# An attention and routed-experts kernel: the last head's row of maxima turned one place later, routing steps moved behind the last maxima, and the ramp's order changed

## The chip, the cores and the metric

The kernel runs on one core of one Trainium2 chip. Its time is the device time of one execution in microseconds (us). A core has five engines that run side by side and wait for each other through semaphores: TensorE (PE) multiplies matrices and writes into PSUM; VectorE (DVE), ScalarE (ACT) and GpSimd (POOL) work element by element; SyncE (SP) issues transfers (DMA). Each engine does its instructions in the order in which the program lists them.

## The reference

Three parts follow each other. Attention with 2 x 8 heads of 768 rows and 64 columns, in which a row sees only the columns of its own hash bucket:

```python
q_bits = (np.einsum('bhsd,dk->bhsk', q, proj) > 0); k_bits = ...   # 6 bits each
mask = q_bucket[:, :, :, None] == k_bucket[:, :, None, :]
scores = np.where(mask, scale * np.matmul(q, k.transpose(0, 1, 3, 2)), -1e9)
attn = np.exp(scores - max); attn = attn / (sum + 1e-9); out = np.matmul(attn, v)
```

Then each of the 1536 rows (512 wide) is routed to one of 8 experts by the largest gate logit and goes through relu(x w1) w2 of that expert; then a layer h = x w_in, h * clip(h + 3, 0, 6) / 6, times w_out.

## The kernel before, in words

The program is written out for each engine in a fixed order by Python code; nothing reorders it. Attention runs in 96 steps k, six for each of 16 heads; step k = 6 h + j treats 128 keys of head h. In a step, `scores(k)` makes on PE two halves of 128 x 384 scores (pst, two matmuls each: high times high parts, then the low parts together with the bits and the row of maxima) and on ACT the exp of each (pf). `high(k)` copies pf to fp16 (phi), nearly always on ACT; `low(k)` makes the remainder pf - phi (plo), on GpSimd, in the last two heads mostly on VectorE. `pv(k)` multiplies phi and plo by the values (psv, 36 matmuls for two steps); it is done for two steps together in each odd step, four and five steps late. `mx(n)` makes, eight steps ahead, the maxima that the exp of a later head needs: two matmuls (psm, three PSUM tiles in turn) and a VectorE reduction (mx) of each. After a head's sixth `mx` a small reduction makes top, and `turn` transposes it on PE (pstop), casts it on VectorE (rm), and sends it as a row by DMA into X, where `scores` of that head reads it. The buffers pf are four: the exp of step k waits until plo of step k - 4 is done.

What else must happen in attention is a list of small steps with due times (`at`, `spread`, `stages`): the head's split into parts (`prep`), sign bits (`bits`, psb on PE, b on VectorE), the scale of each group of four heads (`vmax`, `vscale`: psn and pso on PE, then a chain of tiny VectorE operations am, ex, sc, isw), the splitting of values (`vsplit`, vh), the gate columns (`vgate`: psg, gv), a head's output (`evac`: rd, xp), and the routing of the first half (`route(0)`: ge, jo, pl, jt, rh, ohr; `weigh(0)`: se, gt, rg). A due time of 15 stands between the steps 14.5 and 15; `due(k - 0.5)` runs ahead of the step's scores and `due(k)` behind its sums of values. The table Q holds most of these times. Q["ac"] says how many `mx` the first eight steps do, Q["hn"] how many idle heating matmuls (`heat`, zeros times zeros) stand behind the scores of a step. The ramp is the part before the main loop (scores of steps 0 and 1, the first `vscale`) with the first steps of the loop.

Of the kernel before, what the change touches and what calls it, by code (L numbers as in the profile page):

```python
# [23 lines left out]
NC = S // P  # L24
# [21 lines left out]
LEAD = 8  # L46
# [17 lines left out]
def moe_attention_kernel(ctx, tc, qk, v, vt, pj, wg, w1, w2, win, wout, out, cap):  # L64
# [246 lines left out]
    Q = {'tk': (84, 86), 'v': (-3.25, -4.75, -1.75, -2.25), 'vg': (-6.5, -6.75), 'vgd': 1, 'pr': (-13.0, -12.75, -12.0, -12.5), 'prd': 0.6, 'b0': 7.75, 'b': 1.75, 'bd': 0.5, 'vm0': (9.5, 10.5, 11.5, 12.5), 'vm': (-0.5, 4.75, 7.0, 12.25), 'vs': 13.25, 'pa': 1.5, 'ev': 0.5, 'lvt': -5.0, 'v4': (2.0, 4.25, 10.0, 16.25), 'vg0': (1.85, -4.4, 9.0), 'p2': 3.5, 'lr': (0.25, 1.25, 2.25), 'lv': 4.0, 'vsd': 0.75, 'ac': (1, 1, 3, 5, 6, 7, 8, 10), 'hd': (3, 5, 17), 'hn': (0, 0, 3, 2, 2, 1, 0, 0), 'ap': (0,), 'h0': (7,), 'hl': (6,), 'l0': (), 'll': (1, 3), 'ht': (6, 3, 7, 6, 3, 2)}  # L311
# [4 lines left out]
    with ExitStack() as actx:  # L316
# [486 lines left out]
        run(vs)  # L803
        heat(ps_v, "v", 2)
# [45 lines left out]
        stages(first[1], (2, 3, 3.5, 4, 4.5))  # L850
# [3 lines left out]
        for g in range(1, G):  # L854
            b = 4 * NC * (g - 1)
            spread(b + Q["b"] + (g == 2) if g > 1 else Q["b0"], bits(g), Q["bd"])
            at(b - 6 if g > 1 else Q["lv"], load_v, g)
            for i in range(4):
                at(b + (Q["vm"] if g > 1 else Q["vm0"])[i], vmax, g, i)
            if g == 1:  # L860
                stages(vscale(g), (13, 14.5, 15.25, 16.75, 17.5))
            else:
                spread(b + Q["vs"], vscale(g))
# [19 lines left out]
        stages(route(0, lambda: misc("psr0")), [66 + 1.5 * i for i in range(8)] + [84.5 + 0.75 * i for i in range(14)])  # L883
# [13 lines left out]
        for k in range(STEPS + LAG + 2):  # L897
            due(k - 0.5)
            if 1 < k <= STEPS and not on_dve(k - 1):
                high(k - 1, act)  # L900
            if 1 < k < STEPS:
                scores(k)
# [683 lines left out]
```

## Time and profile before

| | |
|---|---|
| timed runs | 661.88, 658.0, 662.19 us; median 661.88 |
| the profiled execution | 658.55 us, of which the span of its instructions is 656.8 |
| mean granted clock of TensorE | 0.985 of full |
| busy: PE, DVE, ACT, POOL | 96%, 73%, 66%, 36% of the span |
| attention | from the start to about 226 us |
| hand-over to the experts (routing, first gathers) | about 226 to 239 us |

A row of a timeline says when an instruction (or several alike, "x6") began, how long it was busy, its engine, line and operation, "what it writes<-what it reads", the size, and in brackets how long its engine had been idle before it and who released it. A busy PE is not a PE at its peak: its clock has two levels, 1.00 (2.4 GHz) and 0.50 (1.2 GHz) of the granted clock.

### The profile page before, as it was taken

How to read it: one execution, taken by the hardware profiler on the slowest of the kernel's cores; microseconds unless marked ns; L12 is line 12 of the kernel's file. 1: busy time of each engine (PE TensorE's matmuls, PEld its weight loads, DVE VectorE, ACT ScalarE, POOL GpSimd, SP SyncE). 2: the span in 40 equal slices, each digit the busy share in tenths (PEclk: the TensorE clock that was granted, in tenths of full speed). 3: DMA queues.
4: the chain of work that ended last, by engine and by line, in shares of the span. 5: the costliest groups of instructions: out<-in, count | busy, mean ns of one | idle time of the engine just before them, and what ended most of it. 6: DMA issues, size and time to landing. Idle time of an engine off the chain costs nothing.

```text
span 656.8 us, 14463 instructions
## 1 busy us (share of the span) xinstructions
PE 627.4 (96%) x5529; PEld 456.8 (70%) x5529; DVE 477.0 (73%) x1056; ACT 436.6 (66%) x882; POOL 236.0 (36%) x221
## 2 busy tenths in 40 slices
PE   8899999999998889999999999999999999999893
PEld 3578788888887669999999995555555555555441
DVE  6689899998998888888888887888888342222420
ACT  8768878888886847777776755455555586555730
POOL 6567978988995052110666300000000030000011
PEclk9899999999996999999999999999999999999998
DMA  5647758746464168777677643444341010000011
GB/s 195 202 109 222 196 129 230 193 128 164 116 187 157 28 203 300 247 248 230 215 250 258 205 138 107 142 150 139 129 132 61 1 64 33 1 0 1 1 49 53
DMA packets 35732, 92.19 MB, mean 140 GB/s; under 512 B 6778, under 2 KB 12250, under 8 KB 35650
## 3 DMA queue, kind: packets, MB, share of 16 engines
q1 hardware_dynamic: 32562, 83.75, 42.4%
q0 software_dynamic: 2400, 7.36, 3.3%
q8 instruction: 46, 0.75, 0.4%
q14 instruction: 36, 0.29, 0.1%
q10 hardware_dynamic: 688, 0.03, 0.1%
HBM read 67.14 MB, written 6.29 MB: 112 GB/s over the span
## 4 chain that ended last, share of the span: by engine, by line
PE 55%; ACT 3%; DVE 3%; DMA 2%; issue 1%; POOL 0%; POOLq 0%; DVEq 0%
PE psg L1360 17%; PE pso L1387 15%; PE psy L1138 11%; PE psh L1111 11%; DMA out_dram<-os,inv 2%; ACT junk L1314 2%; PE psa L1088 1%; ACT gh L1370 1%; DVE wl L164 1%; DVE rl L1363 1%; ACT rl L1362 0%; PE heat L1190 0%; DVE hl L1115 0%; POOL out_dram L1402 0%; ACT wh L158 0%
## 5 line engine op out<-in xcount | busy, mean ns | idle before, releaser
L493 POOL TENSOR_TENSOR plo<-pf,phi 128x768 f16<-128x768 f32 x86 | 147.0, 1734 | 21.6 <-ACT phi L487 8.1
L1402 POOL DMA_INDIRECT out_dram<-os,inv x12 | 12.2, 1014 | 270.7 <-DVE os L1394 244.3
L482 ACT ACTIVATE pf<-pst 128x384 f32<-128x384 f32 x192 | 83.5, 486 | 37.6 <-PE pst L481 34.6
L459 DVE TENSOR_REDUCE mx<-psm 128x1 f32<-128x384 f32 x192 | 96.2, 546 | 12.4 <-PE psm L456 12.0
L164 DVE SCALAR_TENSOR_TENSOR wl<-raw,wh 128x1024 f16<-128x1024 f32 (+1 forms) x68 | 82.4, 1215 | 6.0 <-ACT wh L158 5.2
L1360 PE MATMUL psg<-yTh,ch 128*128 128x512 f16 (+1 forms) x256 | 83.4, 326 | 3.2 <-DVE rl L1363 3.2
L1360 PE MATMUL psg<-yTl,ch 128*128 128x512 f16 (+1 forms) x256 | 83.4, 326 | 0.0
L1360 PE MATMUL psg<-yTh,cl 128*128 128x512 f16 (+1 forms) x256 | 83.4, 326 | 0.0
L1363 DVE SCALAR_TENSOR_TENSOR rl<-rl,psg 128x512 f32<-128x512 f32 x64 | 35.0, 551 | 64.4 <-ACT rl L1362 64.0
L480 PE MATMUL pst<-Y,K 128*128 128x384 f32 x192 | 76.4, 398 | 2.1 <-ACT pf L482 2.0
L1360 PEld LDWEIGHTS <-ch 128*128 128x128 f16 x512 | 50.1, 98 | 35.9
L487 ACT ACTIVATE phi<-pf 128x768 f16<-128x768 f32 x85 | 71.7, 843 | 1.9
L1387 PE MATMUL pso<-ch,gh 128*128 128x512 f16 x192 | 72.8, 379 | 0.0
L1387 PE MATMUL pso<-ch,gl 128*128 128x512 f16 x192 | 72.8, 379 | 0.0
L1387 PE MATMUL pso<-cl,gh 128*128 128x512 f16 x192 | 72.8, 379 | 0.0
L158 ACT ACTIVATE wh<-raw 128x1024 f16<-128x1024 f32 (+1 forms) x68 | 67.4, 998 | 0.8 <-DVE offs L987 0.8
L481 PE MATMUL pst<-X,K 77*128 77x384 f32 x192 | 66.8, 348 | 0.6 <-DMA X<-rm 0.6
L1387 PEld LDWEIGHTS <-gh 128*128 128x128 f16 x384 | 37.6, 98 | 42.3
L1138 PE MATMUL psy<-hh,wl 128*128 128x224 f16 x256 | 66.3, 259 | 0.2 <-DVE wl L164 0.2
L1138 PE MATMUL psy<-hh,wh 128*128 128x224 f16 x256 | 66.3, 259 | 0.0
L1138 PE MATMUL psy<-hl,wh 128*128 128x224 f16 x256 | 66.3, 259 | 0.0
L508 PE MATMUL psv<-vh,phi 128*128 128x73 f16 x576 | 65.7, 200 | 0.0
(250 smaller groups left out, 1484.7 us busy)
## 6 DMA issues: line engine op xcount, KB each, us to landing
raw<-in_w_dram SPq DMA_DIRECT2D x64, 512.0 KB
rc<-in_win_dram SPq DMA_DIRECT2D x16, 512.0 KB
rc<-in_wout_dram SPq DMA_DIRECT2D x16, 512.0 KB
r<-in_qk_dram SPq DMA_DIRECT2D x16, 384.0 KB
K<-hi SPq DMA_DIRECT2D x26, 192.0 KB
vr<-in_v_dram SPq DMA_DIRECT2D x4, 768.0 KB
vt<-in_vt_dram SPq DMA_DIRECT2D x8, 384.0 KB
K<-lo SPq DMA_DIRECT2D x16, 192.0 KB
```

What stands on the lines that cost most here:

```text
L158: act.activation(wh[e, i][:, c : c + n], r, AF.Copy, scale=(S1, S2)[i // 2])
L164: dve.scalar_tensor_tensor(out=wl[e, i][:, c : c + n], in0=r, scalar=(S1, S2)[i // 2], in1=wh[e, i][:, c : c + n], op0=ALU.mult, op1=ALU.s ...
L459: dve.tensor_reduce(out=mm[:, c, n : n + 1], in_=ps[:, :HS], axis=AX.X, op=ALU.max)
L480: pe.matmul(ps[:, :HS], st["K1"][:, kc], st["Y"][:, qc], start=True, stop=False)
L481: pe.matmul(ps[:, :HS], st["K2"][0:77, kc], st["X"][0:77, qc], start=False, stop=True)
L482: act.activation(pf[:, qc], ps[:, :HS], AF.Exp, scale=0.125 / SC / SC)
L487: act.activation(phi_t[k], pf_t[k], AF.Copy)
L493: eng.tensor_tensor(out=plo_t[k], in0=pf_t.pop(k), in1=phi_t[k], op=ALU.subtract)
L1111: pe.matmul(ps, l[:, c], r[:, k], start=n == 0, stop=n == 3 * KD - 1)
L1138: pe.matmul(ps, l, r, start=n == 0, stop=n == 3 * KF - 1)
L1360: pe.matmul(ps, l, x, start=n == 0, stop=n == 3 * KD - 1)
L1387: pe.matmul(po[blk][s], l, r, start=first and n == 0, stop=last and n == 2)
```

## The change

Six things change, all of them the place of instructions, except for one tiny copy and one more heating matmul in all. (1) `turn` of the last head (n = 95, done in step 87) stands behind that step's `pv` and no longer ahead of it. (2) The steps of `route(0)` from jo on are due later, so that they stand behind the last maxima. (3) A copy of isw onto itself on GpSimd, queued behind the first scale. (4) In the ramp the maxima are spread 1, 2, 2 over steps 2 to 4 in place of 2, 2, 1; the gate columns are made half a step earlier; heating goes from 2 to 1 matmul in steps 3 and 4, and three heating matmuls come ahead of `scores` of step 6. (5) `vscale` of group 1 is due later (13, 15, ...). (6) `bits` of group 2 are due one step earlier.

```diff
--- before.py
+++ after.py
@@ -308,7 +308,7 @@
                 )
 
 
-    Q = {..., 'ac': (1, 1, 3, 5, 6, 7, 8, 10), ..., 'hn': (0, 0, 3, 2, 2, 1, 0, 0), ...}
+    Q = {..., 'ac': (1, 1, 2, 4, 6, 7, 8, 10), ..., 'hn': (0, 0, 3, 1, 1, 1, 0, 0), ...}
 
 
     HT = Q["ht"]
@@ -801,6 +801,7 @@
         next(vs)
         next(vs)
         run(vs)
+        pool.tensor_copy(isw, isw)
         heat(ps_v, "v", 2)
         mx(NC)
         run(pre[1])
@@ -847,18 +848,18 @@
                 at(k, next, gen, None)
 
         stages(first[0], (2, 2))
-        stages(first[1], (2, 3, 3.5, 4, 4.5))
+        stages(first[1], (2, 2.5, 3, 3.5, 4.5))
         at(5.0, run, pre[2])
         for i in range(3):
             at(Q["lr"][i], load_r, 5 + i)
         for g in range(1, G):
             b = 4 * NC * (g - 1)
-            spread(b + Q["b"] + (g == 2) if g > 1 else Q["b0"], bits(g), Q["bd"])
+            spread(b + Q["b"] if g > 1 else Q["b0"], bits(g), Q["bd"])
             at(b - 6 if g > 1 else Q["lv"], load_v, g)
             for i in range(4):
                 at(b + (Q["vm"] if g > 1 else Q["vm0"])[i], vmax, g, i)
             if g == 1:
-                stages(vscale(g), (13, 14.5, 15.25, 16.75, 17.5))
+                stages(vscale(g), (13, 15, 15.75, 17, 17.75))
             else:
                 spread(b + Q["vs"], vscale(g))
         for h in range(8, NH):
@@ -880,7 +881,7 @@
             elif h < NH - 1:
                 at(k + Q["pa"], pair, h // 2)
                 at(NC * h + (-1.9 if h > 1 else -3.5), load_vt, h // 2 + 1)
-        stages(route(0, lambda: misc("psr0")), [66 + 1.5 * i for i in range(8)] + [84.5 + 0.75 * i for i in range(14)])
+        stages(route(0, lambda: misc("psr0")), [66 + 1.5 * i for i in range(8)] + [84.5, 85.25, 87.25, 87.75] + [88.25 + 0.67 * i for i in range(10)])
         stages(weigh(0), (84, 86, 87.25, 88.5, 90.5, 91.5, 92.5))
         stages(any_unmatched(), (88.5, 91, 93.5))
         for i in range(4):
@@ -898,6 +899,8 @@
             due(k - 0.5)
             if 1 < k <= STEPS and not on_dve(k - 1):
                 high(k - 1, act)
+            if k == NC:
+                heat(ps_v, "v", 3)
             if 1 < k < STEPS:
                 scores(k)
             if k < 8 and Q["hn"][k]:
@@ -912,11 +915,11 @@
             for n in AHEAD[k] if k < len(AHEAD) else (k + LEAD,):
                 if n < STEPS:
                     mx(n)
-                if n == STEPS - 1:
-                    turn(turns.pop())
             for u in (k - LAG - 1, k - LAG) if k % 2 else ():
                 if 0 <= u < STEPS:
                     pv(u)
+            if k + LEAD == STEPS - 1:
+                turn(turns.pop())
             due(k)
         assert not later
         for q in range(4):
```

GpSimd at the end of the ramp's preparation, before, and then now (names carry the head or step as their first number; plo0 is the remainder of step 0, vh0 the values of head 0):

```order
L392 TENSOR_TENSOR lo1_242<-rs1_243,hi1_240 128x768
L493 TENSOR_TENSOR plo0_412<-pf0_331,phi0_340 128x768
L733 TENSOR_TENSOR vh0_426<-vr0_179,vh0_426 128x6x64
L493 TENSOR_TENSOR plo1_452<-pf1_349,phi1_397 128x768
L493 TENSOR_TENSOR plo2_483<-pf2_399,phi2_439 128x768
L493 TENSOR_TENSOR plo3_514<-pf3_441,phi3_470 128x768
```

```order
L392 TENSOR_TENSOR lo1_242<-rs1_243,hi1_240 128x768
L804 COPY isw_75<-isw_75 128x1
L493 TENSOR_TENSOR plo0_413<-pf0_331,phi0_340 128x768
L733 TENSOR_TENSOR vh0_421<-vr0_179,vh0_421 128x6x64
L493 TENSOR_TENSOR plo1_448<-pf1_349,phi1_398 128x768
L493 TENSOR_TENSOR plo2_478<-pf2_400,phi2_436 128x768
```

The copy of isw stands ahead of plo0, so plo0 and all behind it wait for the last operation of the scale on VectorE.

PE in the loop's steps 2 and 3, from the second `mx` of head 1 on, before, and then now (psm1cn is half n of chunk c of head 1's maxima, pst3n the scores of step 3, psg0 the gate columns):

```order
L456 MATMUL psm110_414<-K21_145,X1_142 128x384
L456 MATMUL psm111_417<-K21_145,X1_142 128x384
L456 MATMUL psm120_420<-K21_145,X1_142 128x384
L456 MATMUL psm121_423<-K21_145,X1_142 128x384
L571 MATMUL psg0_431<-vt0_182,wg_sb_74 32x256 x3
L480 MATMUL pst30_442<-Y0_139,K10_140 128x384
L481 MATMUL pst30_442<-X0_138,K20_141 128x384
L480 MATMUL pst31_446<-Y0_139,K10_140 128x384
L481 MATMUL pst31_446<-X0_138,K20_141 128x384
L335 LDWEIGHTS idle_sb_135
L335 MATMUL heatv_408<-idle_sb_135 128x512
L335 LDWEIGHTS idle_sb_135
```

```order
L456 MATMUL psm110_415<-K21_145,X1_142 128x384
L456 MATMUL psm111_418<-K21_145,X1_142 128x384
L571 MATMUL psg0_426<-vt0_182,wg_sb_74 32x256 x3
L480 MATMUL pst30_439<-Y0_139,K10_140 128x384
L481 MATMUL pst30_439<-X0_138,K20_141 128x384
L480 MATMUL pst31_443<-Y0_139,K10_140 128x384
L481 MATMUL pst31_443<-X0_138,K20_141 128x384
L335 LDWEIGHTS idle_sb_135
L335 MATMUL heatv_409<-idle_sb_135 128x512
L456 MATMUL psm120_450<-K21_145,X1_142 128x384
L456 MATMUL psm121_453<-K21_145,X1_142 128x384
L456 MATMUL psm130_456<-K21_145,X1_142 128x384
```

Two matmuls of maxima (chunk 2) moved from ahead of the scores of step 3 to behind them, and one heating matmul went.

VectorE at the last maxima (psm1550 and psm1551, chunk 5 of head 15), before, and then now (mx0 and jo are the routing's, se0 the gate's sum, rd13 begins the output of head 13):

```order
L459 TENSOR_REDUCE mx1_161<-psm1540_4179 128x1
L459 TENSOR_REDUCE mx1_161<-psm1541_4182 128x1
L253 TENSOR_REDUCE mx0_3309<-ge0_4163 128x6
L254 TENSOR_TENSOR jo_107<-ge0_4163 128x24
L284 TENSOR_REDUCE se0_4187<-ex0_4103 128x6
L459 TENSOR_REDUCE mx1_161<-psm1550_4202 128x1
L459 TENSOR_REDUCE mx1_161<-psm1551_4205 128x1
L462 TENSOR_REDUCE top_157<-mx1_161 128x6
L468 CAST rm1_159<-pstop15_4209 6x128
L257 SCALAR_TENSOR_TENSOR pl0_4249<-mx0_3309,pos_106 128x6
L259 SCALAR_TENSOR_TENSOR jt0_4251<-tokid_72,jo_107 128x24
L286 TENSOR_SCALAR se0_4187<-se0_4187 128x6
```

```order
L459 TENSOR_REDUCE mx1_161<-psm1540_4181 128x1
L459 TENSOR_REDUCE mx1_161<-psm1541_4184 128x1
L284 TENSOR_REDUCE se0_4187<-ex0_4105 128x6
L459 TENSOR_REDUCE mx1_161<-psm1550_4202 128x1
L459 TENSOR_REDUCE mx1_161<-psm1551_4205 128x1
L462 TENSOR_REDUCE top_157<-mx1_161 128x6
L468 CAST rm1_159<-pstop15_4245 6x128
L253 TENSOR_REDUCE mx0_3311<-ge0_4165 128x6
L254 TENSOR_TENSOR jo_107<-ge0_4165 128x24
L286 TENSOR_SCALAR se0_4187<-se0_4187 128x6
L518 TENSOR_SCALAR rd13_4252<-psv13_4044,sc3_3283 128x6
L521 RECIPROCAL rd13_4252<-rd13_4252 128x6
```

The reduction of ge and jo moved from ahead of the last two maxima to behind the cast of the row; pl and jt moved further back, out of this piece.

PE at the same place: before, the turning ahead of the sums of values, and now the end of these sums, with the turning behind them and ahead of the scores of step 88:

```order
L456 MATMUL psm1550_4202<-K23_153,X3_150 128x384
L456 MATMUL psm1551_4205<-K23_153,X3_150 128x384
L467 MATMUL pstop15_4209<-ident_64,top_157 6x128
L508 LDWEIGHTS phi82_4023
L508 MATMUL psv13_4042<-vh13_3548,phi82_4023 128x73
L509 LDWEIGHTS phi82_4023
```

```order
L510 LDWEIGHTS plo83_4121
L510 MATMUL psv13_4044<-vh13_3550,plo83_4121 128x73
L467 MATMUL pstop15_4245<-ident_64,top_157 6x128
L480 MATMUL pst880_4259<-Y2_147,K12_148 128x384
L481 MATMUL pst880_4259<-X2_146,K22_149 128x384
L480 MATMUL pst881_4263<-Y2_147,K12_148 128x384
```

The 72 rows of loads and matmuls of the sums, which were behind pstop15, are ahead of it.

## Rows read from the trace of the kernel before

**Rows 1.** windows: length, busy PE, PEld, DVE, ACT, POOL, then clock, DMA share, GB/s
```profile
29.10:32.40 3.30, 3.30 (x11) 2.47 (x10) 2.07 (x7) 3.24 (x8) 1.47 (x2) 0.50 0.14 60
...
203.20:213.40 10.20, 9.02 (x85) 7.81 (x85) 7.88 (x24) 4.17 (x8) 3.39 (x5) 0.50 0.48 143
...
226.00:237.00 11.00, 7.04 (x58) 3.52 (x57) 9.35 (x42) 3.85 (x14) 4.84 (x5) 1.00 0.31 83
...
240.00:250.00 10.00, 10.00 (x106) 9.76 (x104) 9.80 (x32) 6.91 (x24) 4.39 (x5) 1.00 0.96 355
```

**Rows 2.** timeline of the ramp, ScalarE
```profile
22.45 0.83 ACT L487 ACTIVATE phi<-pf 128x768 f16<-128x768 f32 x1
...
24.65 0.87 ACT L482 ACTIVATE pf<-pst 128x384 f32<-128x384 f32 x2 [1.37 <-PE pst L481]
...
28.83 0.87 ACT L482 ACTIVATE pf<-pst 128x384 f32<-128x384 f32 x2 [2.43 <-PE pst L481]
...
35.24 0.87 ACT L482 ACTIVATE pf<-pst 128x384 f32<-128x384 f32 x2 [2.02 <-PE pst L481]
```

**Rows 3.** timeline of the ramp, VectorE
```profile
19.48 0.90 DVE L637 TENSOR_SCALAR am<-am 128x2 int32<-128x2 int32 x1
...
20.42 0.17 DVE L638 TENSOR_SCALAR am<-am 128x2 int32<-128x2 int32 x1
...
21.52 2.87 DVE L459 TENSOR_REDUCE mx<-psm 128x1 f32<-128x384 f32 x6
...
27.50 0.41 DVE L577 COPY gv<-psg 96x256 f32<-96x256 f32 x1
...
32.49 0.28 DVE L468 CAST rm<-pstop 6x128 fp32r<-6x128 f32 x1
```

**Rows 4.** timeline of the ramp, PE
```profile
27.96 0.38 PE L581 MATMUL psg<-ident,gv 96*128 96x96 f32 x2 [1.28 <-DVE gv L577]
```

**Rows 5.** timeline of the ramp, GpSimd
```profile
18.71 1.65 POOL L493 TENSOR_TENSOR plo<-pf,phi 128x768 f16<-128x768 f32 x1 [3.42 <-ACT phi L487]
...
22.62 0.90 POOL L733 TENSOR_TENSOR vh<-vr,vh 128x384 f16<-128x384 f32 x1 [2.26 <-ACT vr L729]
```

**Rows 6.** timeline at the last head, VectorE
```profile
202.06 1.02 DVE L254 TENSOR_TENSOR jo<-ge 128x24 f32<-128x24 f32 x1
...
204.16 0.17 DVE L462 TENSOR_REDUCE top<-mx 128x6 f32<-128x18 f32 x1
...
204.80 0.28 DVE L468 CAST rm<-pstop 6x128 fp32r<-6x128 f32 x1 [0.47 <-PE pstop L467]
...
207.01 0.22 DVE L518 TENSOR_SCALAR rd<-psv,sc 128x6 f32<-128x6 f32 x1 [1.69 <-PE psv L510]
...
209.62 0.61 DVE L735 SCALAR_TENSOR_TENSOR vh<-vr,sc,vh 128x384 f16<-128x384 f32 x1
```

**Rows 7.** timeline of the hand-over, VectorE
```profile
229.29 0.17 DVE L254 TENSOR_TENSOR jo<-ge 128x24 f32<-128x24 f32 x1
```

**Rows 8.** timeline at the last head, PE
```profile
204.38 0.38 PE L467 MATMUL pstop<-ident,top 128*6 128x128 f32 x1 [2.29 <-DVE top L462]
```

**Rows 9.** timeline at the last head, ScalarE
```profile
207.80 1.13 ACT L482 ACTIVATE pf<-pst 128x384 f32<-128x384 f32 x2 [4.72 <-PE pst L481]
...
214.32 1.01 ACT L482 ACTIVATE pf<-pst 128x384 f32<-128x384 f32 x2 [0.19 <-PE pst L481]
```

**Rows 10.** timeline at the last head, GpSimd
```profile
201.40 1.64 POOL L493 TENSOR_TENSOR plo<-pf,phi 128x768 f16<-128x768 f32 x1
...
210.47 2.36 POOL L493 TENSOR_TENSOR plo<-pf,phi 128x768 f16<-128x768 f32 x1
```

**Rows 11.** timeline at the scale of group 1, PE
```profile
54.88 0.27 PE L620 MATMUL psn<-ident,am 128*1 128x128 f32 x1 [0.91 <-DVE vh L590]
```

**Rows 12.** timeline at the sign bits of groups 2 and 3, VectorE
```profile
82.30 0.62 DVE L419 TENSOR_SCALAR b<-psb,pj_sb 128x384 fp32r<-128x384 f32 x1 [0.94 <-PE psb L430]
...
131.48 0.62 DVE L419 TENSOR_SCALAR b<-psb,pj_sb 128x384 fp32r<-128x384 f32 x1 [0.42 <-PE psb L430]
```

More of the change, by code (lines that the diff above doesn't have):

```diff
@@ L308, in windows @@
                 )
-    Q = {'tk': (84, 86), 'v': (-3.25, -4.75, -1.75, -2.25), 'vg': (-6.5, -6.75), 'vgd': 1, 'pr': (-13.0, -12.75, -12.0, -12.5), 'prd': 0.6, 'b0': 7.75, 'b': 1.75, 'bd': 0.5, 'vm0': (9.5, 10.5, 11.5, 12.5), 'vm': (-0.5, 4.75, 7.0, 12.25), 'vs': 13.25, 'pa': 1.5, 'ev': 0.5, 'lvt': -5.0, 'v4': (2.0, 4.25, 10.0, 16.25), 'vg0': (1.85, -4.4, 9.0), 'p2': 3.5, 'lr': (0.25, 1.25, 2.25), 'lv': 4.0, 'vsd': 0.75, 'ac': (1, 1, 3, 5, 6, 7, 8, 10), 'hd': (3, 5, 17), 'hn': (0, 0, 3, 2, 2, 1, 0, 0), 'ap': (0,), 'h0': (7,), 'hl': (6,), 'l0': (), 'll': (1, 3), 'ht': (6, 3, 7, 6, 3, 2)}
+    Q = {'tk': (84, 86), 'v': (-3.25, -4.75, -1.75, -2.25), 'vg': (-6.5, -6.75), 'vgd': 1, 'pr': (-13.0, -12.75, -12.0, -12.5), 'prd': 0.6, 'b0': 7.75, 'b': 1.75, 'bd': 0.5, 'vm0': (9.5, 10.5, 11.5, 12.5), 'vm': (-0.5, 4.75, 7.0, 12.25), 'vs': 13.25, 'pa': 1.5, 'ev': 0.5, 'lvt': -5.0, 'v4': (2.0, 4.25, 10.0, 16.25), 'vg0': (1.85, -4.4, 9.0), 'p2': 3.5, 'lr': (0.25, 1.25, 2.25), 'lv': 4.0, 'vsd': 0.75, 'ac': (1, 1, 2, 4, 6, 7, 8, 10), 'hd': (3, 5, 17), 'hn': (0, 0, 3, 1, 1, 1, 0, 0), 'ap': (0,), 'h0': (7,), 'hl': (6,), 'l0': (), 'll': (1, 3), 'ht': (6, 3, 7, 6, 3, 2)}
     HT = Q["ht"]
```

## The prediction

> **What bounds the kernel now.** I read the clock by stretches first, then the idle time of ScalarE, then who ends it. TensorE (PE) runs at the granted 1.00 (2.4 GHz) nearly all the time; it falls to 0.50 (1.2 GHz) in two places of attention: from about 29.1 to 32.4 us in the ramp, and from 203.2 to 213.4 us at the last head [rows 1]. Before both PE had stood still: 1.28 us for VectorE's copy of gv [rows 4], and 2.29 us at the turning of the last head's row, which waits for VectorE's top [rows 8]. In attention PE issues in a fixed order, two score blocks, their maxima, two sums of values, and ScalarE (ACT) does an exp and a copy for each block. So time lost by PE shows as idle time of ACT that ends with pst: 1.37, 2.43 and 2.02 us in the ramp (5.82) [rows 2], and 4.72 us at the last head [rows 9]. PE's order holds no times, only waits, so what a stage gains stays gained unless a later stage is paced by another engine. What follows attention (routing, experts, the last two products) issues in the same order before and after, and I let it move along unchanged.
>
> **Ramp: GpSimd behind the scale.** VectorE's first tensor_scalar on the scale took 0.90 us, the next one, on the same tile and shape, 0.17 [rows 3]. The 0.90 ends at 20.38, and GpSimd's first plo ran from 18.71 to 20.36 [rows 5]. With plo queued behind isw the scale should be done 0.90 - 0.17 = 0.73 us earlier, and the maxima start at 20.8 in place of 21.52. The added copy on GpSimd has one element per partition, and no row has just that; the nearest is far larger, so I count it at 0.1 to 0.2 us. Queued behind it are plo of block 0, the low half of vh and the next plos. Plo 0 then runs from about 21.0 to 22.6, and the low half of vh started only at 22.62 because ACT's vr was late [rows 5]; ACT is busy until then in the new order too. So GpSimd's chain is late by 0.1 us at most: the cover is the 2.26 us that GpSimd idled. Were it gone, plo 0 to 3 and the first sums would move back by as much.
>
> **Ramp: maxima spread otherwise.** Six maxima took 2.87 us, 0.48 each [rows 3]; with three PSUM tiles a fourth matmul of maxima waits for the first reduction.
> (a) Score block 3 stands behind two matmuls fewer: 0.73 + 2 x 0.48 = 1.7 us earlier. ACT was idle 1.37 there, so its exp starts as soon as the copy before it ends (23.28): the whole 1.37 goes [rows 2].
> (b) The copy of gv stood behind ten maxima (27.50); now it stands behind four, 20.8 + 4 x 0.48 = 22.7 at the earliest. Score block 4 stands behind four more maxima and the turning of gv: the last of these matmuls may start after the fifth reduction, 22.7 + 0.41 + 0.48 = 23.6, and with some 1.0 us for it and the turning the block starts near 24.7, where ACT is free at 23.28 + 0.87 + 0.83 = 25.0 [rows 2, 3]. So the 2.43 goes too, and PE's stop of 1.28 with it [rows 4].
> (c) The row of head 1 hangs on VectorE: 23.1, eight more maxima (3.9), four small vh operations and the top, so its cast comes near 28.9 in place of 32.49 [rows 3], 3.6 us earlier. ACT's 2.02 before block 6 stays, since it is the row's way through the transfer; the three added heating matmuls lie in that wait.
> Two heating matmuls go, three come: nothing that PE doesn't have idle. Together the ramp gains what the row gains, **3.5 us**. Bounds: 2.0 if the clock falls here as before (3.3 us at half rate hold back 1.65 us of PE's work), 4.1 if block 6 waits less as well.
>
> **Scale and bits of later groups.** The turning of the second group's maxima moves behind the sums of values. PE stood 0.91 us for it [rows 11]; ACT has other work for half of this, so I take **0.5** (0 to 0.91). The sign bits of group 2 move one step ahead, which is where group 3 has them already; VectorE waited 0.94 us for them in group 2 and 0.42 in group 3 [rows 12]. That is 0.52 of VectorE's time, which is not the bound there: **0.2** (0 to 0.52).
>
> **Last head's row.** PE's last maxima matmul ended near 202.1; then it waited 2.29 us for top, because VectorE did the routing's jo (1.02) ahead of the last two maxima [rows 6, 8]. Now the sums of values come first. Their inputs are there (GpSimd had done the plos of 82 and 83 before it went on to 85 at 201.40 [rows 10]), so PE goes on at 202.1 at full rate. From the turning to the exp of block 88 it took 204.38 to 207.80, 3.42 us at half rate [rows 8, 9], for turning, sums and half a score block; at full rate some 1.7 to 2.0, with the turning behind the sums now. Top is ready in time: without jo and its reduction it starts at 204.16 - 1.2 = 203.0. So exp 88 starts at about 204.1, a gain of 3.7. The row's cast comes near 203.9 in place of 204.80; from cast to the exp that uses the row it took 2.75 us in the ramp (32.49 to 35.24) [rows 2, 3], so exp 90 could start at 206.7; ACT, with its own work, gets there at about 208.2.
> What is late next: exp of block 91 needs the plo of 87, four blocks back, and that stands on GpSimd behind a copy that waits for VectorE's vh of head 15. From cast to vh VectorE took 4.82 us, 1.69 of them waiting for the sums [rows 6]; now 4.82 - 1.69 + 0.3 (jo and its reduction, moved here) = 3.4, so vh starts at 207.3 to 207.9, by single durations the later, in place of 209.62. GpSimd's plo then ends 1.7 to 2.3 us earlier than 212.83 [rows 10], at about 211.0, and exp 91 starts there instead of 214.32 [rows 9]: **3.3 us**. From then on ACT's own work paces the rest. Bounds: 2.3 if only PE's stop goes and the half rate stays; 4.5 if GpSimd's plo is quicker than its 2.36 us, which it spent partly beside VectorE.
> The price of jo at its new place is open from both sides: 1.02 beside GpSimd's plo, 0.17 on the same operation later, with GpSimd idle [rows 6, 7]. GpSimd's plo of 85 ends at 203.04 [rows 10] and the new jo comes at about 204.3, so I take 0.17; with 1.02 everything behind it, and exp 91, would come 0.85 later and the gain be 2.4.
> The Trainium skill (SBUF — State Buffer, section "SBUF: two separate sides") calls the port pair shared by the two engines an exclusive lock that a VectorE operation with two SBUF inputs waits for until GpSimd's instruction ends; the trace agrees, jo ended at 203.08 and plo at 203.04. By that rule jo costs 0.17 and the gain is 3.3; without it 2.4. The same rule speaks against leaving the routing's ge beside an earlier plo, and the change leaves it there, so nothing is regained by it.
>
> **Sum.** 3.5 + 0.5 + 0.2 + 3.3 = 7.5 us, from 4.3 (2.0 + 0 + 0 + 2.3) to 10.0 (4.1 + 0.9 + 0.5 + 4.5). The profiled execution took 658.55 us, so 651.05. The timed runs have 658.0, 661.88 and 662.19: two of them lie 3.3 to 3.6 above the profiled one, with the same program. What they do otherwise isn't shown; another stretch at half rate would do it. The new median may lie at 651.05 or at 661.88 - 7.5 = 654.4; I take the middle, **652.6**.
>
> **Rivals.** (1) The ramp doesn't hand its gain on: the row of head 1 still ends ACT's wait, the clock still falls. For it: fewer heating matmuls (one in place of two) in a stretch where PE waits for VectorE's 0.48 us steps. Against: the stop of 1.28 us, the largest there, goes. Price 2 to 2.5 us: 655.
> (2) At the last head the wait moves instead of going: block 90 waits for its row, turned behind the sums, or GpSimd's plo of 87 doesn't come earlier. For it: the row is then the youngest link, 1.5 us ahead of need by my sum, and plo hangs on VectorE. Against: VectorE stands 1.69 us in that stretch for the sums alone. Gain 1 in place of 3.3: 654.9. With (1) at once, or if the order does nothing at all: 657 to 660.
> (3) Slower: the half rate moves into PE-bound work. At the last head VectorE and GpSimd paced much of the ten microseconds; from 240 us on PE is busy without a break, and in the hand-over before it, 226 to 237 us, it has stops [rows 1]. Ten microseconds at half rate there cost 5, and another 3.3 in the ramp 1.7; with half of the forecast's gain left (3.8) the kernel ends at 658.55 - 3.8 + 6.7 = 661.5, on the median's base 664.8. It decides from 15 us more half rate in PE-bound work than before (15 / 2 = 7.5). Against: the hand-over has heating matmuls and kept 1.00 in this execution.
>
> **Chances.** Forecast 0.62; (1) 0.14, (2) 0.12, both or nothing 0.07, (3) 0.05. A measurement of this kernel can hardly tell 1% (6.6 us) from no change; faster by more is below 655.3: nearly all of the forecast and under half of (1) and (2), 0.66. Slower by over 1%: 0.03. Same: 0.31. The range takes the sum's ends on both bases, 648.55 to 657.6, a little wider below: 647.8 to 657.6.
>
> **What would show it.** Ramp: the first tensor_scalar of the scale near 0.17, no stop of PE above 0.5 us at gv, clock 1.00 from 24 to 33, exp of block 6 near 31.7. Last head: no wait at pstop, ACT's idle time 1 us in place of 4.72, jo near 0.17, clock 1.00 from 200 to 212 of the old time scale. I would be wrong if attention ended earlier by 7 us and the kernel did not, or if PE's stop reappeared at pst of block 90.

## The result and the profile after

The changed kernel takes 652.10 us (median of six runs, 651.15 to 653.98) against 658.57 us for the kernel before in six runs beside them (657.83 to 662.19): a ratio of 0.9891, with a 95% interval of 0.986 to 0.9922, so 5 to 9 us less. Once more, later: 652.33 against 658.56 us, 0.9908 (0.9875 to 0.9942). The prediction was 652.6 us.

The profiled executions are one of each: 658.55 us before and 653.98 after (span 652.3), only 4.57 us apart. Where it came from is read off the starts of the same instructions in both traces, counted from the first instruction of each; minus is earlier in the changed kernel:

| start of | shift, us |
|---|---|
| exp of block 0 | +0.32 |
| exp of blocks 3, 4, 6 | -1.12, -3.02, -3.44 |
| exp of blocks 7, 12 | -2.33, -2.55 |
| exp of blocks 18, 36, 87 | -2.84, -2.77, -2.23 |
| exp of blocks 88, 91, 95 | -6.01, -6.33, -7.14 |
| first and second expert | -5.96, -6.25 |
| end of the last product; end | -6.04, -4.57 |

Four things are to be explained: the ramp gains 3.8 us to block 6 (with block 0 late by 0.32) and hands on 2.9; the last head gains 4.9 (block 87 to 95) and not 3.3; 0.9 us go between block 95 and the second expert; 1.5 us go behind the last product.

The windows of the changed kernel, columns as in [rows 1]; the second is the last head, on the new time scale:

```profile
29.10:32.40 3.30, 3.30 (x48) 2.52 (x46) 3.30 (x5) 1.66 (x4) 3.30 (x3) 1.00 0.07 27
196.00:213.00 17.00, 15.15 (x215) 12.21 (x211) 16.29 (x43) 13.95 (x28) 7.10 (x9) 1.00 0.39 131
226.00:237.00 11.00, 8.17 (x71) 6.20 (x71) 8.34 (x25) 4.11 (x10) 7.50 (x8) 1.00 0.68 202
```

Both stretches at 0.50 are gone. VectorE in the ramp answers to [rows 3]:

```profile
19.81 0.17 DVE L637 TENSOR_SCALAR am<-am 128x2 int32<-128x2 int32 x1
...
23.00 0.41 DVE L577 COPY gv<-psg 96x256 f32<-96x256 f32 x1
...
29.07 0.27 DVE L468 CAST rm<-pstop 6x128 fp32r<-6x128 f32 x1
29.27 1.02 DVE L459 TENSOR_REDUCE mx<-psm 128x1 f32<-128x384 f32 x2
30.21 3.41 DVE L374 SCALAR_TENSOR_TENSOR lo<-r,hi 128x768 fp32r<-128x768 f32 x1
```

The scale's first step takes 0.17 us, gv and the row come 4.5 and 3.4 us earlier. The last line is new trouble: head 2's lo, 0.95 us in the kernel before, takes 3.41. GpSimd's timeline, which answers to [rows 5], shows beside what:

```profile
21.26 0.19 POOL L804 COPY isw<-isw 128x1 f32<-128x1 f32 x1 [5.43 <-DVE isw L649]
21.41 1.65 POOL L493 TENSOR_TENSOR plo<-pf,phi 128x768 f16<-128x768 f32 x1
23.01 0.90 POOL L733 TENSOR_TENSOR vh<-vr,vh 128x384 f16<-128x384 f32 x1
...
29.55 3.25 POOL L493 TENSOR_TENSOR plo<-pf,phi 128x768 f16<-128x768 f32 x2
```

Two plos in a row end at 32.80; lo ends at 33.62, 0.8 us behind them. ScalarE, which answers to [rows 2], pays:

```profile
25.81 0.87 ACT L482 ACTIVATE pf<-pst 128x384 f32<-128x384 f32 x2 [0.56 <-PE pst L481]
...
28.47 0.85 ACT L482 ACTIVATE pf<-pst 128x384 f32<-128x384 f32 x2
...
31.80 0.87 ACT L482 ACTIVATE pf<-pst 128x384 f32<-128x384 f32 x2 [1.61 <-PE pst L481]
33.66 0.84 ACT L370 ACTIVATE hi<-r 128x768 fp32r<-128x768 f32 x1 [0.98 <-DVE vh L738]
```

The waits of 1.37 and 2.43 have shrunk to none and 0.56, the one for the row (2.02) to 1.61. But hi of head 3 uses the buffer that lo of head 2 reads, so it waits 0.98 (the memset that the row names is the operation right behind lo), and block 7 stands behind hi.

The last head, VectorE, GpSimd, ScalarE and PE apart; they answer to [rows 6, 10, 9, 8]:

```profile
200.89 0.17 DVE L462 TENSOR_REDUCE top<-mx 128x6 f32<-128x18 f32 x1
201.43 0.28 DVE L468 CAST rm<-pstop 6x128 fp32r<-6x128 f32 x1 [0.37 <-PE pstop L467]
...
201.72 0.16 DVE L254 TENSOR_TENSOR jo<-ge 128x24 f32<-128x24 f32 x1
...
204.80 0.61 DVE L735 SCALAR_TENSOR_TENSOR vh<-vr,sc,vh 128x384 f16<-128x384 f32 x1
```
```profile
206.29 1.66 POOL L493 TENSOR_TENSOR plo<-pf,phi 128x768 f16<-128x768 f32 x1
```
```profile
201.79 0.87 ACT L482 ACTIVATE pf<-pst 128x384 f32<-128x384 f32 x2 [0.94 <-PE pst L481]
...
207.99 0.87 ACT L482 ACTIVATE pf<-pst 128x384 f32<-128x384 f32 x2 [1.70 <-POOL plo L493]
```
```profile
201.12 0.27 PE L467 MATMUL pstop<-ident,top 128*6 128x128 f32 x1
```

The turning waits for nothing, jo takes 0.16, and ACT's 4.72 us before block 88 are 0.94. The next wait is block 91's, for GpSimd's plo of 87, as named in the prediction.

### The profile page after: what moved, and what is told of

The parts are those of the page before. It is cut to its first block, busy times and chain, and to the rows that moved or that the text cites. A ratio compares the mean times of both kernels' runs of the same rounds, so it can differ in the third digit from the quotient of the medians.

```text
span 652.3 us, 14467 instructions
## 1 busy us (share of the span) xinstructions
PE 623.4 (96%) x5530; PEld 452.5 (69%) x5530; DVE 478.8 (73%) x1056; ACT 435.9 (67%) x882; POOL 234.0 (36%) x222
## 4 chain that ended last, share of the span: by engine, by line
PE 56%; DMA 4%; ACT 3%; issue 1%; DVE 1%; POOL 0%; POOLq 0%; DVEq 0%; ACTq 0%
PE psg L1363 17%; PE pso L1390 15%; PE psy L1141 11%; PE psh L1114 11%; DMA out_dram<-os,inv 3%; ACT junk L1317 2%; PE psa L1091 1%; ACT gh L1373 1%; DVE rl L1366 1%; DMA xg<-xd,ids 1%; DMA xd<-xp 1%; ACT rl L1365 0%; POOL xg L1072 0%; ACT xp L944 0%; POOL out_dram L1405 0%
## 5 line engine op out<-in xcount | busy, mean ns | idle before, releaser
L493 POOL TENSOR_TENSOR plo<-pf,phi 128x768 f16<-128x768 f32 x86 | 145.3, 1713 | 19.7 <-DVE phi L489 10.0
L480 PE MATMUL pst<-Y,K 128*128 128x384 f32 x192 | 74.9, 390 | 2.5 <-ACT pf L482 2.5
L481 PE MATMUL pst<-X,K 77*128 77x384 f32 x192 | 65.4, 341 | 0.6 <-DMA X<-rm 0.6
L508 PE MATMUL psv<-vh,phi 128*128 128x73 f16 x576 | 64.0, 197 | 0.0
```

The costliest lines, as they stand in the source:

```text
L480: pe.matmul(ps[:, :HS], st["K1"][:, kc], st["Y"][:, qc], start=True, stop=False)
L481: pe.matmul(ps[:, :HS], st["K2"][0:77, kc], st["X"][0:77, qc], start=False, stop=True)
L493: eng.tensor_tensor(out=plo_t[k], in0=pf_t.pop(k), in1=phi_t[k], op=ALU.subtract)
```

## The experiments

Eleven runs were made in three groups. Their profiled executions stand in one table, with the changed kernel's first one; each figure is how much longer (+) or shorter (-) a stage lasted than in the profiled kernel before, from one start to the next, with the mean granted clock of the stage in the windows 24 to 40, 198 to 214 and 218 to 238 us (before: 0.89, 0.68, 1.00).

| kernel | ramp: block 0 to 12 | last head: block 87 to 95 | hand-over: block 95 to second expert | behind the last product |
|---|---|---|---|---|
| x1 last head both | +0.30 (0.89) | -4.91 (1.00) | +0.78 (1.00) | -0.24 |
| x2 turn only | -0.68 (1.00) | -4.14 (1.00) | +1.84 (0.91) | +0.08 |
| x3 route only | +1.41 (0.68) | -3.32 (0.89) | +1.82 (0.91) | +1.46 |
| x4 heating in the stop | +1.46 (0.68) | -3.29 (1.00) | +0.76 (1.00) | +1.30 |
| y2 all but last head | -3.45 (1.00) | -1.80 (0.89) | -0.11 (1.00) | -0.25 |
| changed | -2.87 (1.00) | -4.91 (1.00) | +0.89 (1.00) | +1.47 |
| z1 changed again | -3.35 (1.00) | -4.91 (1.00) | +1.83 (0.91) | -0.08 |
| y4 no heating at 6 | -2.87 (1.00) | -4.91 (1.00) | +1.90 (0.91) | -0.05 |
| y3 no copy, old scale | -3.07 (1.00) | -4.90 (1.00) | +2.42 (0.91) | +1.66 |
| y1 lo held, vh early | -3.81 (1.00) | -5.62 (1.00) | +1.24 (1.00) | -0.25 |
| z2 low halves behind gates | -4.23 (1.00) | -5.62 (1.00) | +1.54 (1.00) | +1.07 |
| z3 more heating | -3.81 (1.00) | -5.59 (1.00) | +1.44 (1.00) | -0.14 |

The first four and the kernel before share one program in the ramp, and it lasted up to 2.1 us longer in one execution than in another, with the clock at 0.68 to 1.00. So a single pair of profiles sizes a stage no better than that where the clock can fall; the last column scatters by 1.9 us whatever the order.

The hand-over column holds two things that can be read apart. The first lies at the end of attention, where VectorE makes the last four plos in a row. Its row and ScalarE's with block 95, in the kernel before and then in the changed one:

```profile
220.85 3.68 DVE L493 TENSOR_TENSOR plo<-pf,phi 128x768 f16<-128x768 f32 x4
221.68 0.85 ACT L482 ACTIVATE pf<-pst 128x384 f32<-128x384 f32 x2
```
```profile
214.20 3.67 DVE L493 TENSOR_TENSOR plo<-pf,phi 128x768 f16<-128x768 f32 x4
214.55 0.85 ACT L482 ACTIVATE pf<-pst 128x384 f32<-128x384 f32 x2
```

The plos end 2.85 us behind the start of block 95 before, and 3.32 now. PE's first idle matmul behind attention (heatt) follows them, 3.46 us behind block 95 before and in y2, 3.94 in x1, x2, the changed kernel and z1, 4.57 to 4.59 in y1, z2 and z3. So 0.48 us of the changed kernel's 4.91 are gone by the end of attention. Before, VectorE waited twice for PE's sums on the way there (1.69 us each time, at 207.01 [rows 6] and 219.58); now it has no idle time above 0.1 us from the row's cast at 201.43 to the end of these plos, so it sets the end. The second thing is the clock. From heatt to the second expert the stage took 0.12 us less to 0.41 more than before in the seven executions that kept 1.00, and 1.35 to 1.95 more in the five where the clock fell.

**x1, the last head's part alone.** On the kernel before:

```diff
-                if n == STEPS - 1:
-                    turn(turns.pop())
...
+            if k + LEAD == STEPS - 1:
+                turn(turns.pop())
...
-        stages(route(0, lambda: misc("psr0")), [66 + 1.5 * i for i in range(8)] + [84.5 + 0.75 * i for i in range(14)])
+        stages(route(0, lambda: misc("psr0")), [66 + 1.5 * i for i in range(8)] + [84.5, 85.25, 87.25, 87.75] + [88.25 + 0.67 * i for i in range(10)])
```

> The kernel before with the last head's part of the change alone: the row turned behind that step's sums of values, and the routing's operations at their new places. Theory (the last head carries two thirds of what the change brings, the ramp's gain is mostly given back): block 88's exp some 3 us earlier than before, block 95's 4.5 to 5 us, experts about 4 us, and the time 3.5 to 5 us under the kernel before. Rival (my prediction's sizes: 3.3 here, 3.5 in the ramp): 3.3 us or less. The ramp must read as before, with block 6's exp within 0.2 us of its place.

654.99 against 658.64 us, ratio 0.9942 (0.9923 to 0.9961). Block 88 came 3.8 us earlier, block 95 4.9, the experts 4.1 (all against block 87). The theory's sizes hold, the rival's 3.3 is exceeded. Block 6 was 0.31 off its place against block 0, not 0.2.

**x2, the turning alone** (the first two pieces of that diff).

> The kernel before with the turning of the last row alone moved behind the step's sums of values; the routing's operations stay at their old places, so jo still stands ahead of the last maxima on VectorE. Theory (PE's stop and the half rate behind it are the cause): the sums take some 1.9 us at full rate and cover most of the 2.29 us of the stop, no half rate follows, exp 88 comes 2.5 to 3.5 us earlier and the time falls by 2.5 to 4 us. Rival (VectorE's late work is the cause: jo at 1.02 us and everything behind it): exp 88 moves, but exp 91, which hangs on VectorE's vh of head 15 and GpSimd's low half of 87, moves by 1.7 us at most, and so does the end.

656.92 us, ratio 0.9973 (0.9952 to 0.9994), 1.7 us less. PE's stop at the turning was still 1.06 us, since jo stood ahead of the maxima with 1.03 us, but the clock stayed at 1.00 and the stage lost 4.1 us; block 91 moved by 3.3, twice what the rival allows. In the profiled execution 1.84 us of this went again behind block 95, where the clock fell; the time gained less than the theory's 2.5 to 4 us.

**x3, the routing's places alone** (the last piece of the diff).

> The kernel before with the routing's operations alone at their new places; the row is turned ahead of the sums as before. Theory: jo no longer stands ahead of the last maxima, PE's stop at the turning shrinks from 2.29 to about 1.1 us; if the clock then stays at 1.00 the gain is 2 to 4 us, if it still falls 1.2 us. Rival (the stop in any size is what counts, and order on VectorE is worth nothing by itself): within 1 us of the kernel before.

657.17 us, ratio 0.9978 (0.9953 to 1.0004), 1.5 us less; the interval holds the rival's 1 us too, and no change at all, so the time doesn't decide. The stop shrank to 1.27 us, the clock fell all the same but for a shorter time (0.76 from 203.2 to 208 us, 0.90 to 213.4), and the stage lost 3.3 us. That is beyond the theory's 1.2 us for a clock that falls; it fell for a third as long. The two halves, 4.1 and 3.3, overlap: together they give 4.9.

**x4, heating while PE waits.** On the kernel before:

```diff
                 if n == STEPS - 1:
+                    heat(ps_m, "m", 9)
                     turn(turns.pop())
```

> The kernel before with nine heating matmuls (128x512, some 0.21 us each, 1.9 us) put between the last maxima matmul and the turning of the last row, so that PE waits for VectorE's top while it is busy; nothing else moves. Theory (the half rate behind the stop costs more than the stop): the granted clock stays at 1.00 from 203 to 213 us, and block 88's exp comes some 1.5 to 2 us earlier, block 95's 2 to 3.5 us, though top is as late as before. Rival (the waits are what costs, the clock hardly matters as VectorE and GpSimd pace that stretch): clock 1.00, but block 95 moves by less than 1 us.

657.93 us, ratio 0.9983 (0.996 to 1.0006). In the trace, PE before the turning, then the windows in which the kernel before had 0.50:

```profile
204.01 2.10 PE L335 MATMUL heatm<-idle_sb 128*128 128x512 f16 x9
206.29 0.27 PE L467 MATMUL pstop<-ident,top 128*6 128x128 f32 x1 [0.17 <-DVE top L462]
```
```profile
203.20:208.00 4.80, 4.38 (x50) 2.76 (x50) 3.70 (x13) 1.76 (x4) 1.75 (x2) 1.00 0.01 3
208.00:213.40 5.40, 4.58 (x56) 3.42 (x55) 5.30 (x13) 4.47 (x9) 3.14 (x5) 1.00 0.81 250
```

Nothing moved, PE waits for top as long as before, and yet the stage lasts 3.3 us less: of the 4.9 us that the last head gives against the profiled kernel before, the half rate behind the stop is 3.3. The theory holds for the stage. The time fell by 0.7 to 1.1 us only, and the interval holds no change. One reason shows in the granted clocks of the timed runs: the profiled execution before had more half rate than most. Its mean granted clock was 0.985, the median of the 35 runs of the kernel before beside this one 0.989 (11 of them at 0.985 or less), and 0.992 in the runs of x4. So 3.3 us is the price of some 10 us at half rate in one execution, not what each execution pays; y2 shows one that pays less.

**y2, all but the last head** (the changed kernel with the diff of x1 turned round).

> The changed kernel with the last head's part undone (the row turned ahead of the sums, the routing at its old places); ramp, scale of group 1 and sign bits stay as changed. Theory (what the trace of the changed kernel shows): block 6's exp 3 to 3.5 us earlier than before, block 7's only 2.3, block 18's about 2.8, then PE stops 2.3 us at the last row, the clock falls behind it and the time is 2 to 3 us under the kernel before. Rival (the ramp's gain is only the clock, which falls or not from one execution to the next): block 12 less than 1 us earlier than in the executions of the old ramp that kept the clock at 1.00, and the time within 1 us of the kernel before.

654.43 against 659.2 us, ratio 0.9933 (0.9909 to 0.9958): more than either expected. The ramp kept 3.45 us, 2.8 more than x2's, the old ramp at 1.00, so it isn't the clock alone and the rival falls. The old last head cost 1.8 us less here than in the profiled kernel before, behind the same stop of 2.29 us: the clock was at 0.50 for a shorter time. So against this execution the new last head gains 3.1 us to block 95, and 4.9 against the other. Of the three windows at its stop and behind it, with the columns of [rows 1], only the middle one is at 0.50 throughout:

```profile
200.00:202.00 2.00, 0.64 (x9) 0.58 (x10) 1.50 (x7) 0.06 (x1) 0.01 (x1) 0.85 0.00 0
202.00:204.00 2.00, 2.00 (x33) 2.00 (x31) 0.31 (x5) 0.00 (x0) 0.00 (x0) 0.50 0.10 18
204.00:206.00 2.00, 1.86 (x7) 1.41 (x8) 1.93 (x5) 1.23 (x3) 0.00 (x0) 0.80 0.77 250
```

The parts, 3.65 (x1) and 4.77 us by their medians, add to 8.4, and the whole has 6.2 to 6.5. In the profiles the whole loses 0.9 to 1.8 us behind block 95, x1 0.8 and y2 none; but the parts' intervals (2.6 to 5.1 and 2.8 to 6.0 us) add to 5.4 to 11.0, so it isn't shown by time that the parts give more than the whole.

**y3, without the copy, with the old times of scale and bits.** On the changed kernel:

```diff
-        pool.tensor_copy(isw, isw)
-            spread(b + Q["b"] if g > 1 else Q["b0"], bits(g), Q["bd"])
+            spread(b + Q["b"] + (g == 2) if g > 1 else Q["b0"], bits(g), Q["bd"])
-                stages(vscale(g), (13, 15, 15.75, 17, 17.75))
+                stages(vscale(g), (13, 14.5, 15.25, 16.75, 17.5))
```

> The changed kernel without GpSimd's copy behind the scale, and with the scale of group 1 and the sign bits of group 2 at their old times; the rest stays. Theory: the scale's first tensor_scalar takes about 0.9 us again and the maxima start 0.7 us later, so exp 3, which had no wait, 0 to 0.7 us later and the blocks to 6 as much; at group 1's scale PE's stop of some 0.9 us is back and block 18 loses 0.3; the bits change nothing (under 0.1 us at block 30). Rival (my prediction's sizes): 0.7 in the ramp, 0.5 at the scale, 0.2 at the bits, 1.4 us by block 36.

654.13 us, ratio 0.9915 (0.9886 to 0.9944). VectorE and PE in the trace:

```profile
19.85 0.90 DVE L637 TENSOR_SCALAR am<-am 128x2 int32<-128x2 int32 x1
```
```profile
52.17 0.27 PE L620 MATMUL psn<-ident,am 128*1 128x128 f32 x1 [0.91 <-DVE vh L590]
```

Both old prices are back. Against block 0, block 3 came 0.5 us later than in the changed kernel, blocks 4 and 6 0.7: the copy is worth 0.7 us at block 4, where the other executions with it agree. Further on it can't be told: block 12 came 0.2 later in the changed kernel's first profile than in y3, because of lo, and 0.3 earlier in z1. From block 12 to 30 the stage lasted 0.14 us longer than before, in the executions with the new times 0.21 to 0.40 less: against y3 scale and bits together are worth 0.35 to 0.54 us. The old order itself lasted 0.14 to 0.48 longer there in x1 to x4 than in the profiled kernel before, so against single executions of it the figure lies anywhere from 0.2 to 0.9. From block 24 to 30 alone, where the bits stand, the old order stayed within 0.03 us of the kernel before, and the new one was between 0.38 shorter and 0.13 longer; the executions that gained there had lost as much from block 18 to 24, so the bits' part can't be told from the scale's.

**y4, without the three heating matmuls ahead of block 6.**

> The changed kernel without the three heating matmuls ahead of block 6's scores. Theory (they only fill a wait of PE for the row of head 1, and keep the clock): the granted clock falls to 0.50 somewhere between 30 and 40 us and blocks 7 to 12 come 0.5 to 1.5 us later, or, if the clock holds, no block moves by more than 0.2 us. Rival (they stand in the way): block 6's exp 0.3 to 0.6 us earlier and the clock at 1.00.

652.34 us, ratio 0.9886 (0.9851 to 0.9921). The clock held, no block to 12 moved by more than 0.1 us. The matmuls neither help nor stand in the way here. Lo took 3.44 us, as in the changed kernel.

**y1, lo held and vh early.** On the changed kernel, with lo_t keeping head 2's lo and a small tile gatec:

```diff
         at(5.0, run, pre[2])
+        at(5.75, lambda: pool.tensor_copy(gatec, f32(lo_t[2])[:, 0:1]))
...
         for h in range(1, NH):
+            if h == NH - 1:
+                stages(vsplit(h), (87.6, 87.7))
+                continue
```

> The changed kernel with two more moves, at places that can be read apart in one trace. In the ramp GpSimd gets a copy of one column of head 2's lo, between its plos of blocks 4 and 5, so that it waits for VectorE's lo and VectorE's lo doesn't wait for two plos. At the last head VectorE does the low half of vh of head 15 ahead of the routing's pl, jt, rh, gt and of nm and un. Theory: lo takes 1.0 us from the end of plo 4 and ends near 32.2 us in place of 33.62, ScalarE's hi of head 3 follows it, and the exp of block 7 comes 1.1 us earlier than in the changed kernel; GpSimd's plo 5 moves back by some 1 us and nobody waits for that. vh ends 1.0 us earlier, GpSimd's plo of 87 with it, and the exp of block 91 comes 0.9 to 1.4 us earlier. Together 2 to 2.5 us by the end of attention, some 1 to 2 us in the time (about 650). Rival: PE's order paces both places, or the later plos take the gain: block 12 and block 95 come as in the changed kernel within 0.4 us.

651.91 us, ratio 0.9889 (0.9863 to 0.9916). The trace of y1, GpSimd in the ramp, then VectorE and ScalarE:

```profile
29.77 1.64 POOL L495 TENSOR_TENSOR plo<-pf,phi 128x768 f16<-128x768 f32 x1
32.30 0.18 POOL L855 COPY gatec<-lo 128x1 f32<-128x1 f32 x1 [0.88 <-PE pst L483]
32.43 1.66 POOL L495 TENSOR_TENSOR plo<-pf,phi 128x768 f16<-128x768 f32 x1
```
```profile
30.43 1.80 DVE L375 SCALAR_TENSOR_TENSOR lo<-r,hi 128x768 fp32r<-128x768 f32 x1
```
```profile
32.01 0.87 ACT L484 ACTIVATE pf<-pst 128x384 f32<-128x384 f32 x2 [1.60 <-PE pst L483]
32.77 0.85 ACT L371 ACTIVATE hi<-r 128x768 fp32r<-128x768 f32 x1
...
205.21 0.87 ACT L484 ACTIVATE pf<-pst 128x384 f32<-128x384 f32 x2 [0.55 <-POOL plo L495]
```

Lo waits for one plo, hi for nothing, and block 7 comes 1.12 us earlier than in the changed kernel, each against its block 0. At the last head ACT's 1.70 us for the plo of 87 are 0.55, block 91 comes 1.14 us earlier against block 87, and 0.71 are left by block 95. Both mechanisms are shown. But at the end of attention only 0.05 of the 0.71 are left: heatt is 4.59 us behind block 95 in place of 3.94. VectorE, without idle time there, does the same work in another order. The rival named this (the later plos take the gain), and for the end of attention it holds. By the end of the last product y1 is 2.0 us ahead of the changed kernel's first profile, of which lo gives 0.9 and vh next to nothing; the rest came in stages that the two moves don't touch (0.8 between blocks 30 and 87). By time it can't be told from it (0.9889 beside 0.9891 and 0.9908).

**z1, the changed kernel again.**

> The changed kernel once more, unaltered, beside the next two. What varies from one execution to the next should show itself: the exp of block 7 either follows block 6 at once or comes about 1.1 us late (which engine's lo or plo goes first), and the clock in the hand-over, behind PE's wait of 2 us for rg, is 1.00 or 0.50 for about 4 us (a loss of some 1 us). Theory: time 651 to 654, 6 to 7.5 us under the kernel before. Rival (the first comparison was lucky): less than 5 us.

The time is in the first section. Both variations showed. Lo took 1.80 us here, as in y2, and block 7 followed at once; of the five executions with the new ramp and no hold, two (the changed kernel's first and y4) lost 0.9 us there. And in the hand-over the clock, 1.00 in the first profile, fell behind PE's wait for rg (2.20 us here, 1.97 there; columns of [rows 1]):

```profile
226.00:230.00 4.00, 2.91 (x17) 1.78 (x17) 2.93 (x9) 0.00 (x0) 2.66 (x3) 0.75 0.66 193
230.00:234.00 4.00, 3.80 (x27) 2.64 (x26) 2.09 (x5) 2.13 (x4) 2.39 (x3) 0.82 0.78 236
```

**z2, the low halves behind the gates.** On y1:

```diff
-    low_w(2)
     run(wgen)
+    low_w(2)
```

> The kernel with lo held and vh early, and in the hand-over VectorE's two low halves of weights (wl) moved behind the eight small operations that end in rg. Theory: PE's wait of 2.0 to 2.3 us for rg shrinks to 0.3 to 0.9, the clock can't fall there, and GpSimd's first gather, which in two traces stood behind wl, starts 0.5 to 0.7 us after ids in every execution; expert 0 comes 9 to 9.5 us earlier than before in place of 7.95 and the time is 1 to 2 us under the kernel with lo held and vh early. Rival (the gather's landing sets PE's start on the first expert whatever VectorE does): the wait for rg goes, the wait for xg grows by as much, expert 0 and the time stay within 0.5 us.

651.52 us, ratio 0.9897 (0.9866 to 0.9928). PE in the hand-over:

```profile
224.25 0.34 PE L305 MATMUL psg<-rg,ohr 128*128 128x64 f16 x6 [0.75 <-DVE rg L204]
226.91 0.63 PE L1097 MATMUL psa<-ident,xg 128*128 128x128 f32 x4 [1.03 <-DVE xg L1086]
```

The wait for rg shrank from 2.28 us (y1) to 0.75, and a wait of 1.03 for the gathered rows took its place. The first gather was issued 0.48 us after ids. Expert 0 came 9.02 us earlier than before, which the theory had named, but z2 was 0.7 us ahead of y1 at block 95 already: counted from there expert 0 gained 0.3, and the second expert lost 0.3. The time didn't fall. So the rival fits better: with rg early PE waits for the gathered rows.

**z3, more heating in the hand-over.** On y1, Q["ht"] (6, 3, 15, 6, 3, 2) in place of (6, 3, 7, 6, 3, 2).

> The kernel with lo held and vh early, with 15 heating matmuls in place of 7 ahead of PE's wait for rg in the hand-over (8 more of 0.21 us, 1.7 us, inside a wait of 2.0 to 2.3); VectorE and GpSimd keep their order. Theory (half rate behind that wait is what some executions lose): the clock is 1.00 from 220 to 240 us, expert 0 in the profile as before within 0.3 us, the slowest of the timed runs come down by about 1 us and the median by 0 to 1. Rival (the clock there costs nothing, since the gather paces it): median and slowest unchanged.

652.74 us (650.07 to 654.12), ratio 0.9908 (0.9875 to 0.9941). The clock was 1.00, but neither the median nor the slowest run came down. What the clock costs there, from heatt to the second expert, is the step from a mean of 0.25 us (-0.12 to 0.41, at 1.00) to one of 1.57 (1.35 to 1.95, fallen): about 1.3 us in an execution in which it falls. A comparison of the medians of six runs doesn't show it.

None of y1, z2 and z3 is shown to beat the changed kernel by time, though their profiled spans (648.5, 649.2 and 648.5 us) are shorter than 652.3 and 650.6.

## Why the prediction was right

**The sum.** Predicted 7.5 us on the profiled execution's time; the medians differ by 6.5 and 6.2, 1.0 and 1.3 short of it. That the time came out only 0.5 and 0.3 us under the forecast of 652.6 is partly luck, of the base (below; the middle of 651.05 and 654.4 is also 652.7). Of the terms the last head's was too small for the execution that it was read from, that of scale and bits too large and the ramp's about right; what lo, the end of attention and the hand-over take wasn't priced.

**Ramp, 3.5.** The steps are in the trace, but for 0.56 us that block 4 still waits for PE: the scale's 0.17, the copy's 0.19 (0.1 to 0.2 forecast), no stop of PE above 0.30 us at gv, block 6 at 31.80 (31.7 forecast) and the row's cast at 29.07 (28.9). Handed on to block 12 were 2.87, 3.35 and 3.45 us in three executions (changed, z1, y2). What the prediction left out is lo: between VectorE and GpSimd the ramp now has a race that costs 0.9 us when two plos go first. The old ramp too varies; against the mean of its five executions (+0.50) the three new ones (mean -3.22) gain 3.7. Rival (1) came only in this small part, and with another mechanism than it named.

**Scale 0.5, bits 0.2.** Together 0.35 to 0.54 us against y3, where 0.7 was forecast. PE's 0.91 at psn went, y3 brought it back; VectorE's wait for the bits fell from 0.94 [rows 12] to 0.32; what that alone gave stays open.

**Last head, 3.3: the mis-sized term.** Block 88 came 3.8 us earlier (3.7 forecast), block 91 4.1 and block 95 4.9, in five executions of the new order that agree within 0.02. The step that was off is "what is late next": I kept GpSimd's plo of 87 at its 2.36 us beside VectorE and had vh start between 207.3 and 207.9. On the old time scale of this stage (2.23 us later) vh started at 207.0, and plo took 1.66. That is the upper bound's case (4.5 at block 91). The last 0.8 lies behind block 91, where I had let ACT's own work pace the rest; x4, which only kept the clock, shows 0.75 of it. In the new order VectorE is without idle time from the row's cast on, and by the end of attention 4.4 of the 4.9 are left. All this is against one execution of the old order; against y2's it is 3.1 at block 95 and 2.6 at the end of attention, and x1 gained 3.65 in time. So the forecast of 3.3 lies within what the old order's own spread leaves open. By the rule of the Trainium skill (SBUF — State Buffer, section "SBUF: two separate sides") jo costs 0.17 at its new place, with GpSimd idle; the trace agrees, 0.16. Of the mechanism, x4 shows the half rate to be the larger part in an execution that has 10 us of it.

**Not priced: the end of attention, and rival (3) in small.** The step that failed is that everything behind attention would move along unchanged. Between block 95 and the second expert the changed kernel lost 0.9 us in one execution and 1.8 in the other. In both 0.48 of it is VectorE's four plos at the end of attention: a later stage paced by another engine, which the prediction allowed for in general and didn't look for here. The rest is 0.4 where the clock stayed at 1.00 and 1.35 where it fell. Behind PE's wait of 2.0 to 2.3 us for rg it fell in five of the eleven executions that have this wait (x2, x3, y3, y4, z1), in none of them for more than a few microseconds. That is rival (3), at about 1.3 us where it had priced 6.7. The kernel before has the same wait (2.21 us) and kept 1.00 in its one profile, so that the change brings the fall isn't shown. With the clock at 1.00 the hand-over varied by 0.5 us; z2 says that PE waits for the gathered rows when rg is early, and what makes these land later wasn't tried.

**The tail.** GpSimd's last rows:

```profile
639.19 0.96 POOL L1405 DMA_INDIRECT out_dram<-os,inv  x1 [2.81 <-DMA out_dram<-os,inv]
644.94 0.96 POOL L1405 DMA_INDIRECT out_dram<-os,inv  x1 [4.79 <-DMA out_dram<-os,inv]
```

Each write of the output waits for the one before it to land, 2.8 us in one case and 4.8 in the next. By the table what stands behind the last product varies by 1.9 us with no order in it. So the profiled pair shows 1.5 us less gain than the program has.

**The base.** More runs put the kernel before at 658.57, 658.64, 659.2 and 658.56 us, where its profiled execution lay (658.55), not at the 661.88 of the first three. From that base the sum gives 651.1; the middle of two bases hid that the sum was 1 us too large. Between blocks 30 and 87 the changed kernel's first profile lost another 0.53 us, z1 only 0.06; that wasn't followed (all eight executions with the new ramp: 0.33 us shorter to 0.53 longer than before).

## What to carry to other kernels

Where PE stands still, look at the clock in the next ten microseconds before pricing the stop: at the last head some 10 us at half rate cost 3.3 us in the execution that had them, and nine idle matmuls in the stop, without any reordering, took that back. When one engine's wait goes, see which engine has no idle time left at the end of the stage: here VectorE kept 0.48 us of the last head's gain, and all of what y1 added but 0.05. When two engines share a path to memory, moving one instruction moves the place of every long pair behind it; a one-column copy in the slower engine's queue settles which goes first. And size a stage from several executions, or from a stage in which neither the clock nor such a race is open: the new last head, at 1.00, repeated within 0.02 us; the old one, where the clock fell for longer or shorter, differed by 1.8, and the ramp and the tail by 2.

## What the runs showed of the hardware

The clock fell or didn't fall at the same stop of the same program: the old ramp ran at 1.00 in x2 and at 0.68 in x3 and x4; behind the 2 us wait for rg the changed kernel kept 1.00 once and fell once (0.75 in the mean from 226 to 230 us). The Trainium skill (TensorE: Matmul & The Clock Gate, section "Part 1: The HAM clock gate (the "warmup" mystery)") has the chip's watch on PE run freely, not from the kernel's start; that fits, but no run here varied the moment of a stop alone.

VectorE's lo, 0.95 us in the kernel before, took 1.80 us when it went between two plos and 3.41 and 3.44 when two stood in a row, although it was ready before the second began. Which of the two happened differed between executions of one program. And GpSimd's tiny copy of vh took 0.89 us at the last head of the changed kernel, beside VectorE's plo of 0.95, and 0.21 in y1, where it came earlier.
